# Tap matmuls of 128 contiguous weights at half-step offsets, and first loads in one ring, in a fused state-space and expert kernel

## The chip, the cores and the metric

The kernel runs on one core of one Trainium2 chip. The metric is the device time of one execution in microseconds, the median of several. A run more than 1.5% above the fastest of its kernel is called slow; with one core this label rests on the time alone. A ratio below is the mean time of one kernel's fast runs over that of the kernel before in the same rounds, so it is not quite the ratio of the medians that stand beside it. The experiments ran on several chips of one kind (the control ran on one of them); on these the kernel before had medians of 207.7 to 210.6 us, on the first chip 212.1. That spread is larger than some of the effects, so I look at the traces as well as at the times. Each trace is one execution.

Short names: PE is TensorE, ACT ScalarE, DVE VectorE, POOL the engine whose queue starts some loads, SP the engine whose queue starts most. A chunk's KT is the tap product moved out of PSUM by ACT (an **eviction**); U and K2T are the spectra of input and taps, PAB their products, which reuse the memory of AT, a table that is stored to DRAM first.

## The reference, cut to what matters

```python
xn = layernorm(u)                                         # 2048 x 512
# state-space branch: one kernel of 2048 taps per channel, used as a long convolution
P  = exp(dt * A[:, :, None] * l)                          # 512 channels x 128 states x 2048
K  = einsum("dn,dnl,dn->dl", C, P, dt * B).real
y  = irfft(rfft(xn, 4096) * rfft(K, 4096))[:2048] + xn * Dskip
# expert branch: the token with the highest router value alone goes through a small gated MLP
r  = xn @ w_r;  token = argmax(r)
xe = xn;  xe[token] += sigmoid(r[token]) * mlp(xn[token])
out = u + y * silu(xe)
```

The kernel doesn't form 2048 taps. It evaluates K at 20 centres times 32 offsets around each (GG holds the centre powers, QQ the offset powers, both complex, 128 states on the partitions) and multiplies the two with matmuls: the **tap matmuls**. The table W then carries the 640 values per channel to a spectrum.

## The kernel before

Work goes in eight **chunks** of 64 channels (two to a pair, four pairs) and four **spectra** that follow the pairs. This is one chunk:

```python
for jj in range(16):
    for ci in range(2):                                   # real, imaginary
        for gp in range(4):                               # channel groups: 4 x 32 weight columns
            mms.append((PB[32*gp:32*gp+32, 4, 20*jj:20*jj+20],
                        QQ[:, qb, ci, gp, 0:32, jj],      # 32 weights, 16 elements apart
                        GG[:, 0, ci, :, 32*gp + 16*js + jj], ci == 0, ci == 1))
...                                                       # KP product on DVE, two more matmuls
act(KT[:, js], PB[:, 4, 0:320]..., Copy, 320)             # first eviction
...                                                       # 16 + 1 "spread" matmuls with IDENT
act(KT2[...].rearrange("p t (c g) -> p g t c", g=4), PB[:, 4, 0:320]..., Copy, 320)   # second, step of 4
```

All instructions stand in a fixed order on each engine (a list, `_ORDER`), semaphores join the engines, and a list `_FILL` puts matmuls without use ("fillers") on PE to keep its clock up. X, the input, is loaded by ACT's queue; sixteen warm-up matmuls run at the start:

```python
for q in range(4):
    xl = g.dma(AC, [xsrc[q]])                             # X in four loads of 512 KB, ACT's queue
...
for k in range(4):                                        # warm-up
    g.M([(PB[:, 6 + k % 2, :], AT[:, 0, 0:128], warm, True, True) for _ in range(4)])
```

## Time and profile before

| | kernel before |
|---|---|
| median, first chip | 212.09 us (209.36 to 212.58, 4 runs) |
| profiled execution | 208.72 us, span 206.6, mean granted clock 0.878 |
| PE / DVE / ACT busy | 175.7 / 142.6 / 136.2 us |
| tap matmuls | 1024 pairs of weight load and matmul, 2.24 us per chunk |
| tap evictions per chunk | 0.44 us, then 0.88 us for the second |
| instruction blocks fetched | 25 packets, 0.41 MB |
| "issue" pauses over 1 us in the chain | 3.11 + 1.56 + 1.20 + 2.05 + 2.71 = 10.63 us |

The page gives the sums; the place of a pause is only in the chain in order of time. The lines themselves are in the prediction below.

### The profile page before, as it was taken

What the parts mean: (1) busy time and instruction counts of PE and PEld (TensorE: products, weight loads), DVE (VectorE), ACT (ScalarE), POOL (GpSimd) and SP (SyncE); (2) the same over time, 40 slices, a digit from 0 to 9 for tenths busy, and PEclk for the clock granted to TensorE, in tenths of its full rate; (3) what the DMA queues carried; (4) which work ended last, traced back from release to release, by engine and by line L of the source; (5) the groups of instructions that cost most, each with busy time, mean ns of one, the idle gap of its engine ahead of it and who ended that gap; (6) DMA issues with size and microseconds to landing.
All of it is one profiled execution on the core that took longest, in us unless ns stands there. A gap on an engine that the chain in (4) does not pass through costs nothing.

```text
span 206.6 us, 7069 instructions
## 1 busy us (share of the span) xinstructions
PE 175.7 (85%) x3170; PEld 127.9 (62%) x3181; DVE 142.6 (69%) x344; ACT 136.2 (66%) x164; POOL 13.9 (7%) x24
## 2 busy tenths in 40 slices
PE   6099998889993999967999998999999649999960
PEld 2044547555883766946898875876799327895420
DVE  1599589997970789801699999959999205542634
ACT  2059589997703978661799999986688422566431
POOL 0074000000000203000000000200002400000000
PEclk9999999995555589985999999889999757999997
DMA  6989972225595692980037297441349852366874
GB/s 176 347 272 405 415 292 84 86 83 156 138 297 185 175 293 51 408 370 8 18 87 205 75 261 198 127 112 33 75 105 306 191 123 51 94 195 178 189 167 102
DMA packets 40528, 36.85 MB, mean 178 GB/s; under 512 B 26577, under 2 KB 35922, under 8 KB 39602
## 3 DMA queue, kind: packets, MB, share of 16 engines
q1 hardware_dynamic: 37458, 20.12, 35.7%
q0 software_dynamic: 2464, 14.19, 19.5%
q10 hardware_dynamic: 576, 2.10, 3.1%
q8 instruction: 25, 0.41, 0.8%
q14 instruction: 5, 0.04, 0.1%
HBM read 25.91 MB, written 10.49 MB: 176 GB/s over the span
## 4 chain that ended last, share of the span: by engine, by line
PE 60%; ACT 12%; DVE 10%; issue 8%; DMA 7%; SPq 0%; DVEq 0%
PE PB L187 58%; DMA STG<-in_A_A_re_dram 3%; ACT U L740 3%; DMA DD<-scr_z 3%; ACT K2T L740 2%; PE PB L275 2%; DVE TT L711 2%; DVE XN L720 2%; ACT QQ L740 2%; ACT ZT L740 1%; DMA scr_z<-ZT 1%; DVE ZB L711 1%; ACT KT L740 1%; ACT XN L740 1%; DVE T L711 1%
## 5 line engine op out<-in xcount | busy, mean ns | idle before, releaser
L187 PE MATMUL PB<-KT,W 128*128 128x128 bf16 x640 | 40.1, 224 | 0.7 <-ACT KT L740 0.4
L187 PEld LDWEIGHTS PB<-KT,W 128*128 128x128 bf16 x640 | 37.3, 100 | 4.2 <-ACT KT L740 1.6
L187 PE MATMUL PB<-CA,AD 32*128 32x256 bf16 (+1 forms) x192 | 24.9, 309 | 5.7 <-DVE AD L724 5.0
L711 DVE TENSOR_TENSOR TT<-GG,ZB 128x512 bf16<-128x512 bf16 (+2 forms) x64 | 27.7, 469 | 0.4
L711 DVE TENSOR_TENSOR PAB<-U,K2T 128x1024 bf16<-128x1024 bf16 x32 | 21.3, 685 | 8.6 <-ACT K2T L740 8.6
L740 ACT ACTIVATE K2T<-PB 128x1024 bf16<-128x1024 f32 x16 | 16.5, 1034 | 14.5 <-PE PB L187 14.4
L187 PEld LDWEIGHTS PB<-CA,AD 32*128 32x128 bf16 x192 | 15.5, 114 | 15.7 <-DVE AD L724 5.9
L711 DVE TENSOR_TENSOR QQ<-QQ,EE 128x2048 bf16<-128x2048 bf16 x16 | 19.5, 1220 | 7.1 <-ACT QQ L740 7.0
L740 ACT ACTIVATE KT<-PB 128x320 bf16<-128x320 f32 x16 | 10.7, 671 | 20.2 <-PE PB L187 20.2
L187 PE MATMUL PB<-GG,QQ 128*32 128x20 bf16 x1024 | 19.8, 223 | 3.9 <-issue 3.9
L187 PEld LDWEIGHTS PB<-GG,QQ 128*32 128x32 bf16 x1024 | 18.8, 170 | 6.3 <-issue 4.3
L187 PE MATMUL PB<-PAB,FA 64*128 64x128 bf16 x512 | 17.9, 222 | 0.6 <-ACT ZT L740 0.4
L740 ACT ACTIVATE U<-PB 128x1024 bf16<-128x1024 f32 x16 | 16.3, 1037 | 2.6 <-PE PB L187 2.6
L740 ACT ACTIVATE ZT<-PB 128x1024 bf16<-128x1024 f32 x16 | 16.5, 1033 | 2.0 <-PE PB L187 2.0
L740 ACT ACTIVATE EE<-PB 128x1024 bf16<-128x1024 f32 x16 | 15.5, 1029 | 2.2 <-PE PB L187 2.2
L187 PEld LDWEIGHTS PB<-PAB,FA 64*128 64x128 bf16 x512 | 15.1, 97 | 3.0 <-ACT ZT L740 0.8
L740 ACT ACTIVATE AT<-PB 128x1024 bf16<-128x1024 f32 x16 | 16.5, 1085 | 0.7 <-PE PB L187 0.7
L711 DVE TENSOR_TENSOR TF<-PB,XN 128x512 bf16<-128x512 f32 x12 | 8.1, 686 | 11.9 <-PE PB L187 8.3
L275 PE MATMUL PB<-CA 128*128 128x512 bf16 x47 | 15.1, 439 | 1.3 <-issue 1.2
L711 DVE TENSOR_TENSOR GG<-TT 128x512 bf16<-128x512 bf16 (+2 forms) x32 | 15.0, 469 | 0.4
L187 PE MATMUL PB<-XN,CB 128*128 128x256 bf16 (+1 forms) x80 | 14.4, 314 | 0.6 <-DVE XN L720 0.5
L187 PE MATMUL PB<-BT,F2T 128*64 128x256 bf16 x128 | 11.3, 307 | 1.9 <-issue 1.6
(131 smaller groups left out, 226.7 us busy)
## 6 DMA issues: line engine op xcount, KB each, us to landing
W<-c_w POOLq DMA_DIRECT2D x4, 1280.0 KB, 9.0
scr_a<-AT SPq DMA_DIRECT2D x8, 512.0 KB, 3.6
BT<-scr_a SPq DMA_DIRECT2D x8, 512.0 KB, 5.0
scr_z<-ZT SPq DMA_DIRECT2D x16, 256.0 KB, 3.4
DD<-scr_z SPq DMA_DIRECT2D x6, 512.0 KB, 5.0
X<-in_A_u_dram ACTq DMA_DIRECT2D x4, 512.0 KB, 7.0
XR<-in_A_u_dram POOLq DMA_DIRECT2D x4, 512.0 KB, 6.3
out_dram<-XR SPq DMA_DIRECT2D x8, 256.0 KB, 3.1
```

What stands on the lines that cost most here:

```text
L187: fns.append(lambda e, o=o, l=l, r=r, st=st, sp=sp, tp=tp: e.matmul(o, lhsT=l, rhs=r, start=st, stop=sp, tile_position=tp, skip_group_chec ...
L275: n.fns = [lambda e, o=o: e.matmul(o, lhsT=lhs, rhs=rhs, start=True, stop=True, tile_position=(0, 0), skip_group_check=True)] * k
L711: g.V(lambda e: e.tensor_tensor(out=o, in0=a, in1=b, op=op), [o], [a, b], n, mode)
L720: g.V(lambda e: e.tensor_scalar(out=o, in0=a, scalar1=s1, scalar2=s2, op0=op, op1=op2), [o], ins + ([s2] if not isinstance(s2, (int, float ...
L740: nd = g.A(lambda e: e.activation(out=o, in_=i, func=func, **kw), [o], ins, n + (110 if "bias" in kw else 0), after=[ph["pre"]] if tab els ...
```

## The change

Its intent: take the offsets at half steps (0.5, 1.5, ...), so that 32 values lie evenly around a centre, and lay QQ out with channels in natural order. Then one tap matmul serves four channels with 128 contiguous weights: 32 pairs of 80 columns instead of 128 pairs of 20. Only a quarter of the 128 x 80 product is wanted; the spread matmuls pick it out. In return the first eviction is four times as large (1280 columns instead of 320, in three groups), and the second one becomes contiguous.

```diff
-            for jj in range(16):
-                for ci in range(2):
-                    for gp in range(4):
-                        mms.append((PB[32 * gp:32 * gp + 32, 4, 20 * jj:20 * jj + 20], QQ[:, qb, ci, gp, 0:32, jj], ...
+            for nj, bank in ((6, 4), (5, 5), (5, 4)):
+                mms = []
+                for k in range(nj):
+                    jj = j0 + k
+                    for ci in range(2):
+                        mms.append((PB[:, bank, 80 * k:80 * k + 80], sap(QQ, ..., [[1, 128]]),
+                                    sap(GG, ..., [[128, 20], [1, 4]]), ci == 0, ci == 1))
+                g.M(mms)
+                act(KT[:, :, j0:j0 + nj], PB[:, bank, 0:80 * nj].rearrange("p (a b) -> p b a", b=80), ACT.Copy, 80 * nj)
+                j0 += nj
...
-            act(KT2[...].rearrange("p t (c g) -> p g t c", g=4), PB[:, 4, 0:320]..., ACT.Copy, 320)
+            act(KT2[:, q, :, 64 * js:64 * js + 64], PB[:, 5, 0:320].rearrange("p (t c) -> p t c", t=5), ACT.Copy, 320)
...
-        for q in range(4):
-            xl = g.dma(AC, [xsrc[q]])
+        for q in range(5):
+            xl = g.dma(SP, [xsrc[q]])        # 256 KB first, in the same ring as A_re and the constants
...
-        g.sec = "warm"                       # the warm-up matmuls go
```

Cut away: the tables for the new offsets, the skip weight (now added by two small fp32 matmuls per half), a new `_FILL` (33 fillers instead of 57), and a whole new `_ORDER` on every engine.

## The prediction

> **What bounds the kernel now.** I read the page from the top, then the chain that ended last in order of time, then the engines' busy times by stretch, then the matmul and ScalarE (ACT) timelines around the part that changes, building the convolution kernel from its "taps".
>
> ```profile
> PE 175.7 (85%) x3170; PEld 127.9 (62%) x3181; DVE 142.6 (69%) x344; ACT 136.2 (66%) x164; POOL 13.9 (7%) x24
> ...
> q8 instruction: 25, 0.41, 0.8%
> ...
> PE 60%; ACT 12%; DVE 10%; issue 8%; DMA 7%; SPq 0%; DVEq 0%
> ...
> L740 ACT ACTIVATE KT<-PB 128x320 bf16<-128x320 f32 x16 | 10.7, 671 | 20.2 <-PE PB L187 20.2
> L187 PE MATMUL PB<-GG,QQ 128*32 128x20 bf16 x1024 | 19.8, 223 | 3.9 <-issue 3.9
> ```
>
> TensorE (PE) carries 60% of the chain. A third of all its matmuls are the 1024 tap matmuls, 20 columns each. "Issue", waiting for nothing that the profile shows, is 8% of the chain, and the tap row itself names it. In the chain by time:
>
> ```profile
> 1.20 6.41 DMA STG<-in_A_A_re_dram
> ...
> 10.07 7.85 PE PB L187 x39
> ...
> 18.25 1.91 PE PB L275 x4
> ...
> 62.08 3.11 issue
> ...
> 88.58 1.56 issue
> ...
> 93.59 1.20 issue
> ...
> 160.56 2.05 issue
> ...
> 166.20 2.71 issue
> ```
>
> The reader is to see two things. The start hangs on the load of A_re, which lands at 7.61 us. Five pauses sum to 10.63 us, each within or just after a block of 128 tap matmuls. By stretch (columns: PE, PEld, DVE, ACT, POOL busy with counts, granted clock, DMA share, GB/s):
>
> ```profile
> 47.00:62.00 15.00, 15.00 (x292) 11.35 (x292) 11.93 (x36) 7.82 (x11) 0.00 (x0) 0.50 0.66 195
> 62.00:75.00 13.00, 9.67 (x230) 6.90 (x228) 6.54 (x14) 8.26 (x11) 1.49 (x2) 0.53 0.68 201
> 110.00:133.00 23.00, 21.69 (x446) 17.41 (x444) 22.69 (x48) 22.62 (x25) 1.18 (x1) 0.98 0.61 167
> 150.00:172.00 22.00, 16.88 (x480) 13.25 (x480) 12.73 (x27) 12.84 (x17) 3.45 (x3) 0.79 0.68 170
> ```
>
> From 47 to 72 us PE is at half clock; from 110 to 133 ACT and VectorE (DVE) are both full, so there a lighter PE buys nothing.
>
> **What the Trainium skill says.** (1) "Runtime: NRT & Kernel Launch", Instruction fetch mechanics: instructions come in 16 KiB blocks of 256, the cost "mostly hidden". The trace agrees on the blocks: 0.41 MB in 25 packets is 16 KB each, and 3170 + 3181 PE instructions at 64 B are 0.41 MB. It disagrees on "hidden", as I read it: in all five pauses one q8 packet starts at most about 2 us before the pause or in its first microsecond, with the DMA busy, and PE resumes some 2 us after it. Two such blocks are 256 tap matmuls, 4.5 us of PE time. (2) "TensorE: Matmul & The Clock Gate", Weight-path perf modes: the fast weight load needs 128 weights and no fp32. The taps before load 32 strided columns, after it 128 contiguous ones. In the trace 64 pairs with 128 contiguous columns and a one-column matmul (RB,XN) take 1.89 us even at half clock, 27 ns each, so a wide load is cheap. (3) "ScalarE: Activation LUTs", What ACT_TABLE_LOAD costs: an ACTIVATE is 186 ns + 0.833 ns per element, so 453 ns for 320. The trace: the first eviction of a chunk takes 0.44 to 0.52 us, the second, which writes at a step of four elements, 0.85 to 0.89 (next fence). (4) "DMA: Bandwidth & Descriptors", Issuing engines are not separate DMA queues: all queues interleave on the same 16 engines. The trace agrees: a 128 KB load takes 6.4 us while 2 MB of X runs beside it from ACT's queue.
>
> ```profile
> 95.45 0.51 ACT L740 ACTIVATE KT<-PB 128x320 bf16<-128x320 f32 x1
> ...
> 100.18 0.88 ACT L740 ACTIVATE KT<-PB 128x320 bf16<-128x320 f32 x1
> ...
> 59.06 2.42 PE L187 MATMUL PB<-GG,QQ 128*32 128x20 bf16 x128
> 61.30 0.27 PE L187 MATMUL PB<-KP,CB 128*4 128x64 bf16 x2
> ...
> 95.67 3.55 PE L187 MATMUL PB<-KT,W 128*128 128x128 bf16 x40
> ```
>
> **The change part by part.** PE instructions fall from 3179 to 2407 matmuls, each with its load (counted in the program).
>
> *Tap matmuls.* Eight chunks. Before, 128 pairs take 61.30 - 59.06 = 2.24 us, 17.5 ns a pair, the same at both clocks. After, 32 pairs of 80 columns. The price of a pair: 40 KT,W pairs (128 columns) usually take 2.41 us at full clock, less one 0.22 us latency over 39 gaps, 56 ns; scaled by 80/128 that is 35 ns, above the 27 ns floor. 32 x 35 = 1.1 us, a gain of 1.1 per chunk at full clock; at half clock 2.2 us, no gain. Six of the eight chunks run mostly at full clock: **-6.5 us**, nearly all on the PE chain.
>
> *Spread matmuls.* Before 16 + 1 per chunk in about 0.4 us; after 20 + 1 + 2 (the two KP matmuls move here), say 0.05 us more each: **+0.4 us**.
>
> *Fetch pauses.* A chunk's tap instructions drop from 256 to 64 and their rate from one per 9 ns to one per 18. Blocks fall from 25 to 19. I expect 2 to 3 of the 10.63 us to stay: **-8 us**.
>
> *Loads.* X leaves ACT's queue; the sync ring carries 256 KB of X, the step sizes, A_re, the first constants, then the rest. 385 KB lie up to and with A_re; at the 347 GB/s of the second slice that is 1.1 us, after an issue near 1.6 us and a landing of about 2 us: A_re near 4.7 instead of 7.61. The PE order also drops the warm-up matmuls (three groups of 1.9 us between 11 and 24 us, between the exponent arguments). The new order puts fillers elsewhere. But DVE needs 16 statistics of 0.68 us = 10.9 and then the normalisations, and is full from 30 to 47. I credit 4.5 of the some 5 to 6: **-4.5 us**.
>
> *Half clock.* Fillers move to the router and the expert (57 become 33, warm-ups apart). Whether they hold the clock I can't tell: **-1.5 us**.
>
> *ACT.* A chunk's tap eviction becomes three, of 480, 400 and 400 elements: 0.58 + 0.52 + 0.52 = 1.62 us for 0.44. Its second eviction becomes contiguous: 0.44 for 0.88. The KE eviction (0.44 every second chunk) becomes one of 64 per chunk, 0.24. Net +0.76 x 8 = 6.1, and two evictions for the skip weight, 2 x 0.4: ACT goes from 136 to about 143 us. The chain runs through ACT between 117 and 142 and two chunks lie there: **+2 us**. The two skip products in fp32 (four passes of 256 columns, estimated): **+0.5 us**. DVE keeps its work but for four memsets: 0.
>
> Sum: -6.5 + 0.4 - 8 - 4.5 - 1.5 + 2 + 0.5 = -17.6. 212.5 - 17.6 = **195 us**.
>
> **The rivals.** *ACT becomes the bound.* The new tap evictions write runs of 5 or 6 bf16 values, at a step of 32 bytes. The step-4 write above costs (880 - 190)/320 = 2.2 ns per element; if short runs pay that, a chunk adds 1280 x 1.3 = 1.7 us more, 13 over eight, and ACT reaches some 156 us. For it: the 0.88 us rows, and 98% ACT in the stretch 110 to 133. Against: runs are not single elements, and ACT is idle some 40% around most chunks. About half would show: 201 us. *The pauses stay.* They may need only a busy DMA, not dense instructions: the pause at 88.58 has DMA share 1.0 all round it. Then only 2 or 3 us of the 8 come: 200 us. *DVE holds the start.* It is busy 16.93 of 17 us between 30 and 47; if its chain, not the load, sets the router's start, 2 of the 4.5 us come: 197 us. *The clock drops more often*, since with fewer tap matmuls and fillers PE idles more: each 10 us of PE work at half clock costs up to 5 us: 200 us or more. *Better than thought:* the tap chain also gets shorter, its evictions running beside the next matmul group, and the spectra start earlier: 187 us.
>
> **Range and chances.** Two rivals at once give about 206, the good one with full credit for pauses and start 186. So 195, range 186 to 206. Faster by over 2% means below 208.3, which needs most gains to fail: 0.93 faster, 0.06 same, 0.01 slower.
>
> **What would show it.** The tap row at 256 matmuls with 32 of them starting within 1.2 us at full clock (wrong: 1.8 or more); issue in the chain at or below 3% for 8; A_re landing before 5.5 us and the first argument matmul before 8; the spread evictions all at 0.44 us and the tap evictions at 0.5 to 0.6 (rival: 0.8 to 1.2); ACT busy 140 to 146 us; QQ products on DVE still at 1.22 us although their runs shrink from 256 to 16 elements. The prediction falls if ACT or DVE carries over 25% of the chain, or if the half-clock stretch grows past 25 us.

## The result, and the profile after

The changed kernel takes **200.32 us** (199.73 to 200.49, 4 runs) where the kernel before takes 212.09: ratio 0.951, 95% interval 0.942 to 0.961. Its direction and range were as predicted; by the medians it gained 11.8 us where 17.6 were expected. Two of the four runs of the kernel before count as slow; by fast runs alone the gain is 10.3 us (210.5 to 200.2). The profiled execution has a span of 198.6 us for 206.6, at a mean granted clock of 0.925 for 0.878; these two traces thus differ by 8.0 us, and only that can be followed in them.

These are the lines of the changed kernel's page that answer to those of before (busy times; fetched instructions; shares of the chain; then groups: line, engine, operation, output and inputs, count, busy us, mean ns of one, idle time before):

```profile
PE 165.8 (83%) x2411; PEld 120.2 (61%) x2411; DVE 143.5 (72%) x339; ACT 144.7 (73%) x186; POOL 13.9 (7%) x24
...
q8 instruction: 19, 0.31, 0.6%
...
PE 36%; DVE 21%; ACT 18%; DMA 17%; issue 2%; SPq 2%; DVEq 0%; ACTq 0%
...
L725 DVE TENSOR_TENSOR QQ<-QQ,EE 128x2048 bf16<-128x2048 bf16 x16 | 19.5, 1219 | 0.2
L187 PE MATMUL PB<-GG,QQ 128*128 128x80 bf16 x256 | 14.2, 213 | 1.4 <-ACT XSEL L754 0.7
```

PE lost 10 us of work and much of the chain (60% to 36%), the pauses left the chain (8% to 2%), and DMA rose from 7% to 17%. In the chain in order of time most of that DMA is one store in the expert's time:

```profile
61.33 0.37 SPq L210
61.74 1.01 SPq L210
62.79 20.52 DMA scr_a<-AT
...
83.40 0.69 DVE PAB L725
```

A store of 512 KB takes 20.5 us here, because the loads of the expert and of W run beside it (8.1 MB were moved between 57 and 80 us, from the windows' rates; in a_pool below, with one of these loads moved away, it takes 10); the products PAB are written over AT's memory, so the first of them waits for it.

More telling than any share are landmarks, the same piece of work in each trace (us; from the timelines). The control is the changed kernel once more, on a later chip; the last two columns belong to experiments below.

| landmark | before | after | control | a_all | a_best |
|---|---|---|---|---|---|
| first argument matmul | 10.1 | 6.5 | 6.9 | 6.5 | 6.5 |
| first matmul on normalised X | 30.2 | 24.9 | 24.6 | 22.2 | 24.8 |
| last of the expert's up matmuls starts | 66.7 | 56.4 | 54.5 | 56.9 | 57.1 |
| first spectrum starts on PE | 80.2 | 78.8 | 77.9 | 81.9 | 75.1 |
| second set of power products starts on DVE | 102.7 | 101.8 | 100.3 | 103.9 | 99.6 |
| first taps of the fifth chunk | 130.4 | 132.6 | 131.1 | 132.3 | 128.0 |
| third spectrum starts | 142.3 | 143.1 | 141.6 | 142.5 | 138.2 |
| fourth spectrum starts | 172.2 | 165.7 | 164.3 | 165.1 | 160.8 |
| last DD matmul group | 199.2 | 190.7 | 189.3 | 190.2 | 186.5 |
| span | 206.6 | 198.6 | 197.2 | 199.2 | 195.6 |

Read down the second and third columns. The changed kernel is 10 us ahead at 56 us, 1.4 us ahead at the first spectrum (79 us), 1 us ahead at 102, 2 us *behind* at 131, and then gains again: 7.3 us of the final 8 between the third and the fourth spectrum, where the kernel before has its last two pauses. The two stretches that decide this, by windows (columns: length; PE, PEld, DVE, ACT, POOL busy; granted clock; DMA share; GB/s), before:

```profile
102.00:124.00 22.00, 21.53 (x382) 18.53 (x383) 21.45 (x48) 21.50 (x23) 0.00 (x0) 1.00 0.56 152
124.00:131.00 7.00, 6.23 (x132) 4.31 (x128) 6.90 (x15) 7.00 (x8) 0.00 (x0) 1.00 0.73 203
160.00:172.00 12.00, 6.88 (x184) 3.85 (x179) 2.94 (x8) 4.26 (x7) 2.29 (x2) 0.62 0.61 137
```

and after:

```profile
102.00:124.00 22.00, 18.96 (x293) 14.47 (x290) 21.80 (x51) 21.45 (x24) 0.00 (x0) 1.00 0.59 172
124.00:131.00 7.00, 7.00 (x85) 4.76 (x86) 5.76 (x11) 5.40 (x6) 1.18 (x1) 0.54 0.60 169
160.00:172.00 12.00, 9.62 (x218) 8.27 (x214) 5.39 (x11) 6.76 (x12) 2.29 (x2) 1.00 0.58 133
```

From 102 to 124 DVE is full in both kernels (21.45 and 21.80 of 22 us), and ACT nearly as full (21.50 and 21.45); in the changed kernel the chain runs over DVE from 101.75 to 123.41 us. Lighter PE work buys nothing there, it only makes PE wait. After the wait PE runs at half clock from 124 to 131 (0.54), where before it ran at full clock. From 160 to 172 it is the other way round: before, the pauses left PE 6.9 of 12 us of work, and the clock fell to 0.62.

### The profile page after: what moved, and what is told of

The parts are those of the page before. It is cut to its first block, busy times and chain, and to the rows that moved or that the text cites. A ratio compares the mean times of both kernels' runs of the same rounds, so it can differ in the third digit from the quotient of the medians.

```text
span 198.6 us, 5566 instructions
## 1 busy us (share of the span) xinstructions
PE 165.8 (83%) x2411; PEld 120.2 (61%) x2411; DVE 143.5 (72%) x339; ACT 144.7 (73%) x186; POOL 13.9 (7%) x24
## 4 chain that ended last, share of the span: by engine, by line
PE 36%; DVE 21%; ACT 18%; DMA 17%; issue 2%; SPq 2%; DVEq 0%; ACTq 0%
PE PB L187 33%; DMA scr_a<-AT 10%; ACT AT L754 4%; ACT XT L957 4%; DVE TT L725 4%; DVE PAB L725 4%; ACT KT L754 4%; DMA X<-in_A_u_dram 3%; DVE ST L802 3%; DVE GG L725 2%; SPq L210 2%; DMA DD<-scr_z 2%; PE PB L280 2%; ACT K2T L754 2%; ACT QQ L754 2%
## 5 line engine op out<-in xcount | busy, mean ns | idle before, releaser
L187 PEld LDWEIGHTS PB<-KT,W 128*128 128x128 bf16 x640 | 35.9, 98 | 6.1 <-ACT K2T L754 3.4
L187 PE MATMUL PB<-CA,AD 32*128 32x256 bf16 (+1 forms) x192 | 25.9, 357 | 9.9 <-DVE AD L738 8.2
L725 DVE TENSOR_TENSOR PAB<-U,K2T 128x1024 bf16<-128x1024 bf16 x32 | 21.2, 685 | 12.8 <-ACT K2T L754 11.8
L187 PEld LDWEIGHTS PB<-CA,AD 32*128 32x128 bf16 x192 | 17.4, 129 | 16.7 <-DVE AD L738 9.1
L754 ACT ACTIVATE KT<-PB 128x400 bf16<-128x400 f32 (+2 forms) x32 | 18.4, 576 | 5.9 <-PE PB L187 5.2
L187 PE MATMUL PB<-GG,QQ 128*128 128x80 bf16 x256 | 14.2, 213 | 1.4 <-ACT XSEL L754 0.7
L187 PE MATMUL PB<-DD,CB 128*128 128x512 bf16 x32 | 10.9, 458 | 4.4 <-DVE TF L725 2.3
L187 PEld LDWEIGHTS PB<-GG,QQ 128*128 128x128 bf16 x256 | 11.9, 106 | 4.0 <-ACT XSEL L754 1.0
L187 PE MATMUL PB<-XN,CB 128*128 128x256 bf16 (+1 forms) x80 | 12.8, 297 | 1.3 <-ACT AT L754 1.3
L802 DVE BATCH_NORM_STATS2 ST<-X 128x6 f32<-128x512 bf16 x16 | 9.9, 683 | 5.1 <-DMA X<-in_A_u_dram 5.1
L280 PE MATMUL PB<-CA 128*128 128x512 bf16 x33 | 13.3, 524 | 0.1
```

The lines of the kernel that those rows point to most:

```text
L187: fns.append(lambda e, o=o, l=l, r=r, st=st, sp=sp, tp=tp: e.matmul(o, lhsT=l, rhs=r, start=st, stop=sp, tile_position=tp, skip_group_chec ...
L280: n.fns = [lambda e, o=o: e.matmul(o, lhsT=lhs, rhs=rhs, start=True, stop=True, tile_position=(0, 0), skip_group_check=True)] * k
L725: g.V(lambda e: e.tensor_tensor(out=o, in0=a, in1=b, op=op), [o], [a, b], n, mode)
L754: nd = g.A(lambda e: e.activation(out=o, in_=i, func=func, **kw), [o], ins, n + (110 if "bias" in kw else 0), after=[ph["pre"]] if tab els ...
L802: g.V(lambda e, b=b: e.bn_stats(ST[:, b, :], X0[:, b, :]), [ST[:, b, :]], [X0[:, b, :]], 512)
```

## The experiments

Twelve runs; the labels with a_ start from the changed kernel, b_ from the one before. Theory: the pauses of the instruction fetch are what the change really removes, and the rest of the gain is given back at later waits. Rivals: it is PE time that counts; the loads; ACT's larger evictions; the DMA burst.

### The loads: a_ring and b_ring

```diff
# a_ring
-            xl = g.dma(SP, [xsrc[q]])
+            xl = g.dma(AC, [xsrc[q]])
# b_ring
-            xl = g.dma(AC, [xsrc[q]])      # four pieces
+            xl = g.dma(SP, [xsrc[q]])      # five pieces, SP's order as in the changed kernel
```

> The changed kernel with one part undone: the loads of X go through the ScalarE-issued ring again instead of ahead of the others in the SyncE ring; nothing else differs. Theory A (the prediction's start term): the early start is worth what it gained at the first argument matmul, 3 to 4.5 us at the end, so about 203 to 205 us. Theory B (the lead is given back before the first spectrum, which in the changed kernel starts only 1.4 us earlier than before although the LayerNorm tail ended 10 us earlier): the first argument matmul moves from 6.5 us back towards 10 us, but the end moves by less than 1 us, 200 to 201 us.

> The kernel before with one part of the change alone: X in five pieces through the SyncE-issued ring in the changed kernel's order, warm-ups and taps as before. Theory A (prediction's start term): about 3 to 4 us faster than before, 208 to 209 us. Theory B (early lead is given back at later waits): within 1 us of before, 211 to 213 us, with the first argument matmul still some 3 us earlier than before's 10.07.

a_ring: 201.59 us, ratio 0.968 (0.960 to 0.977); the control had 0.958 (0.951 to 0.964) on the same chip. The first argument matmul moves from 6.9 to 7.9 us, but the first matmul on normalised X stays (24.7) and the last up matmul starts no later (54.6 for 54.5). It falls behind only between 55 and 80 us, in a stretch that the moved loads don't touch. So theory A's reason is not borne out by a_ring, even if a loss of up to 2 us stands in the times (more than theory B allowed). b_ring: 209.31 us against 208.73, no gain, and its first argument matmul still starts at 9.8 us. The expectation of 3 us there was a miss, and the trace says why: in the order of before a statistics instruction on X stands ahead of the last argument products on DVE and waits for X until 8.6 us. So no gain of the loads alone is shown; that DVE's new order is what they lack is my reading of that wait, and no run tests it.

### The pauses: a_narrow, a_pad, a_narrow2, a_tiny

The question is whether the gain is PE time or instruction density. a_narrow puts the density back with the real sums, a_pad puts PE time back without density:

```diff
# a_narrow
-   mms.append((PB[:, bank, 80*k:80*k+80], QQ[... 128 columns], GG[... [[128, 20], [1, 4]]]))
+   for ch in range(4):
+       mms.append((PB[32*ch: +32, 80*k + ch, step 4, 20 columns], QQ[... 32 columns], GG[... + ch, [[128, 20]]]))
# a_pad, ahead of the first group of a chunk
+   mms = [(PB[:, bank, :], IDENT, CA[:, 0:512], True, True)] * 5
```

> The changed kernel with each 128-column tap matmul split into four of a quarter of the columns: same sums, same order of everything else, but 128 pairs of matmuls per chunk as in the kernel before, so both the PE time of the taps (about 1 us more per chunk, 8 chunks) and the instruction count come back. Theory A (prediction): PE time 6.5 us and fetch pauses 8 us both return, 210 to 215 us, with one-packet instruction blocks about 25 and issue pauses of over 1 us on PE. Theory B (the pauses were off the path or hidden, only PE time counts): 204 to 207 us.

> The changed kernel with five 512-column matmuls without use put ahead of each chunk's taps: 5 x 0.216 = 1.08 us of PE more per chunk at full clock, 8.6 us in all, like the narrow taps, but with only 10 instructions more per chunk. Theory A (PE bounds the chunk loop): nearly all of it shows, 206 to 209 us, instruction blocks 19 to 21, no issue pause over 1 us; what the narrow taps lose beyond this is the fetch pauses. Theory B (the loop is bound by DVE and ACT, PE has slack): under 203 us.

a_pad: fast runs 205.94 and 205.27 us (three others were slow), ratio 0.987 (0.976 to 0.998), that is 6 us above the control's mean of 199.7 for 8.6 us of fillers. Its trace, of a slow run, has 19 blocks and no pause over 1 us on PE. PE time counts, some 70% of it; the intervals of the two ratios allow 40% to all.

a_narrow: 208.3 and 207.2 us in its fast runs, between the bands of theory B (204 to 207) and A (210 to 215), and a trap. Its DVE was busy 155.7 us instead of 143.5 and its ACT 154.0 instead of 144.7, with the same instructions. I blamed the writes to every fourth PSUM column and mended that in a_narrow2 (20 neighbouring columns, as the kernel before writes them):

> The narrow taps again, mended: the first version wrote columns 4 apart in PSUM, and DVE and ACT instructions beside its taps took up to twice their time (2.4 instead of 1.2 us). This one writes 20 neighbouring columns, as the kernel before did. Expected: DVE and ACT durations as in the changed kernel (products of 1.22 us). Then theory A (fetch pauses count): blocks 25, issue pauses over 1 us on the chain, 4 us or more above the version with five fillers per chunk, that is 9 to 12 us above the control. Theory B (only PE time counts): as the fillers, 5 to 8 us above the control, or less.

It took 212.8 and 215.8 us in its fast runs and showed the same stretching. In its timeline (start, duration):

```profile
167.24 1.02 PE L187 MATMUL PB<-GG,QQ 128*32 128x20 bf16 x45
167.34 2.06 ACT L754 ACTIVATE K2T<-PB 128x1024 bf16<-128x1024 f32 x1
167.90 1.90 DVE L725 TENSOR_TENSOR QQ<-QQ,EE 128x2048 bf16<-128x2048 bf16 x1
```

K2T normally takes 1.02 us and the product 1.22; both are stretched while the small tap matmuls run. So my reading of the first version was wrong (it wasn't the PSUM step), and neither run measures what the pauses cost. They do show something else: both fetch 25 blocks, as the kernel before, yet PE's longest pause without a wait is 0.87 us in a_narrow and under 0.35 us in a_narrow2. More blocks alone don't bring the pauses. Alone on PE, 128 narrow pairs take 2.8 us here and took 2.24 us in the kernel before; whether this lower rate is the reason is open. The kernel before has the same number of small tap matmuls and no such stretching (its products stay between 1.20 and 1.23 us); they differ in how the operands lie in memory, and which of these matters is open.

a_tiny asks again without touching QQ and GG, with 96 small matmuls on constants:

```diff
+   mms = [(PB[32*(k%4): +32, bank, 0:20], IDENT[:, 0:32], CA[:, 0:20], True, True) for k in range(96)]
```

> The changed kernel with 96 tiny matmuls (32 weight columns, 20 columns, no result that anyone uses) ahead of each chunk's taps: instruction density as in the kernel before (128 pairs per chunk), and as the narrow taps took about 20 ns a pair, some 1.9 us of PE per chunk, 15 us in all; the operands are constants, so the slowdown of DVE and ACT beside the narrow taps should be absent if it comes from reading GG and QQ in small pieces, and present if it comes from the dense stream of small matmuls itself. The version with five fillers added 8 us of PE and cost about 6 us. Theory A (fetch pauses count): blocks about 25, pauses of over 1 us on PE beyond the PE time, more than 14 us above the changed kernel (over 213 us). Theory B (only PE time counts): 9 to 12 us above (208 to 211).

It took **209.34 us**, all four runs fast: ratio 1.016, the whole gain of the change is gone. DVE and ACT keep their times (143.9 and 144.8), so the dense stream alone doesn't stretch them. The extra PE time came out smaller than I had expected, 0.85 us per chunk (134.56 to 135.41 us in the trace) and not 1.9, so 7 us in all, less than in a_pad; by a_pad's slope of 0.7 that is worth 5 us. It lost 9.8 us over the control's median and 12 us by the ratios of the fast runs (1.016 and 0.958). The rest is 5 to 7 us, and the trace has pauses of about that size. Its page, and its chain by time:

```profile
q8 instruction: 25, 0.41, 0.8%
```

```profile
57.63 0.80 issue
...
77.16 0.40 issue
...
95.76 1.39 issue
...
164.47 0.70 issue
...
167.17 1.83 issue
```

The blocks are back at 25 and the pauses with them: 0.80 + 0.40 + 1.39 + 0.70 + 1.83 = 5.1 us; PE has no such pause over 0.35 us in the control. They belong to the fetch by their time: in all ten pauses, five before and five here, one instruction packet (q8) starts 2.2 to 3.0 us before PE resumes. The numeric bands I had set fit theory B (208 to 211), but only because they assumed too much PE time; pauses present, and less PE time than a_pad at a higher total, speak for theory A. How much of the loss they are is less sure: the slope of 0.7 rests on two fast runs, and a_pad and a_tiny ran on different chips (a_store, of about the control's speed, had 199.9 us on a_tiny's). By landmarks a_tiny is 0.8 us behind the control at the first spectrum, 3.4 at the second power products, 5.1 at the third spectrum and 8.9 at the fourth. The 3.8 us between the last two hold 2.5 us of pauses and two chunks' small matmuls, 1.7 us.

### ACT's evictions: a_again (control) and a_evict

> The changed kernel itself, as the control for its variants on this chip. Nothing is changed, so about 200.3 us and 0.951 of the kernel before if the chip is like the first one; the other chip seen since ran the kernel before at 208.7 instead of 212.1, and then 197 to 199.

> The changed kernel with the taps of a chunk grouped 6, 6, 4 instead of 6, 5, 5: same matmuls, but the second eviction starts and ends on whole pairs of its target. The changed kernel's evictions took 0.57 (480 columns), 0.78 (400 columns, odd run) and 0.54 us (400 columns). Theory A (the odd run is what costs 0.78): 0.57, 0.57 and about 0.47 us, so 0.28 us less per chunk, 2.2 us of ACT in all, and 0 to 1 us off the end. Theory B (bank or order, not the odd run): the second stays near 0.78 or above, and nothing is gained.

The control: 199.59 us (198.52 to 201.21), ratio 0.958. The tap evictions of the changed kernel by form:

```profile
L754 ACT ACTIVATE KT<-PB 128x400 bf16<-128x400 f32 x16 | 10.3, 645 | 1.0 <-PE PB L187 0.5
L754 ACT ACTIVATE KT<-PB 128x480 bf16<-128x480 f32 x8 | 4.6, 570 | 2.7 <-PE PB L187 2.5
L754 ACT ACTIVATE KT<-PB 128x320 bf16<-128x320 f32 x8 | 3.6, 444 | 2.2 <-PE PB L187 2.2
```

The 400-column form takes longer than the 480-column one: half of them 0.78 us, half about 0.53. Grouped 6, 6, 4 (`for nj, bank in ((6, 4), (6, 5), (4, 4))`):

```profile
L754 ACT ACTIVATE KT<-PB 128x480 bf16<-128x480 f32 x16 | 9.3, 581 | 4.4 <-PE PB L187 4.2
L754 ACT ACTIVATE KT<-PB 128x320 bf16<-128x320 f32 x16 | 7.1, 443 | 3.0 <-PE PB L187 2.6
```

The slow form is gone, so it is the group's place and length and not the bank (the second group is still in bank 5): theory A for the duration, 2.0 us of ACT saved by these rows. (The 320 row also holds the eight spread evictions; this trace is of a slow run.) In time: 196.83 us median (193.98 to 200.27), two runs fast, ratio 0.935 (0.925 to 0.945). That is more than 2 us of ACT can give, and the next kernel that contains the same grouping, a_store, had 199.89 us and 0.960. A gain at the end is therefore not shown.

### Where the lead went: a_pool, a_store, a_all

```diff
# a_pool: POOL's order
-   ..., 19, 215, 214, 220, 235, 18, 244, ...
+   ..., 19, 18, 215, 214, 220, 235, 244, ...      # W0 ahead of WD; W0 is part of the table W
# a_store: grouping 6, 6, 4, and SP's order
-   ..., 308, 327, 323, 318, 313, ...              # the store that is ready last stands first
+   ..., 308, 327, 313, 318, 323, ...
# a_all: a_store, and the expert's last part behind the taps, in creation and on PE, ACT and DVE
-   expert(); patch(); loads of W2, W3; kpair(0)
+   expert(); kpair(0); expert_b(); patch(); loads of W2, W3
```

> The changed kernel with one load moved: W0 of the expert (issued at 58.4 us, after WD, in the changed kernel) goes out ahead of WD, as early as its memory is free, so the DMA burst of 57 to 83 us loses 1.3 MB of its 8 MB or so. Theory A (the lead of 10 us at 57 us was lost to the DMA burst: the store of AT took 18 to 20 us to land and the first PAB waited for it): the store lands earlier, the first spectrum starts 2 to 4 us earlier than 78.8 and the end comes 1 to 3 us earlier than the control. Theory B (the lead was lost to the order of work on PE, ACT and DVE in 60 to 72 us, not to DMA): the store lands earlier, but the first spectrum stays at 78 to 80 us and the end within 1 us of the control.

> The changed kernel with taps grouped 6, 6, 4 (as in the run before) and one order changed: the last three stores of AT go out in the order in which ACT finishes them; in the changed kernel the last one to be ready, at 61.3 us, stands first and holds the two others, which then land only at 83.35 us in the DMA burst, and the first PAB products, in AT's memory, wait for that. Theory A (that wait held the first spectrum): no such wait on the chain, first PAB matmul 1 us or more earlier than 83.9 to 84.3, end 1 to 2 us below the 6, 6, 4 version (which was at 0.935 of the kernel before). Theory B (K2T, from the taps by way of PE and ACT, comes at the same time anyway): first PAB matmul within 0.7 us, end within 1 us.

> As the run before it (6, 6, 4 and stores in order of readiness), and the expert's last part and the patch go behind the taps of the first two chunks in the order of every engine, two fillers dropped. Theory A (the 10 us lead at 57 us was lost because the patch, which waits for WD until 65 us, stands ahead of the taps): the spread of the second chunk ends some 8 us earlier, the first spectrum starts at 69 to 73 us instead of 77.6 to 78.8, and the end comes 3 to 6 us earlier: 191 to 194 us where the changed kernel has 199.6. Theory B (the DMA burst of 57 to 83 us or DVE's chains hold the spectra anyway): the first spectrum starts earlier, but the first product of the fourth chunk pair's taps and the end move by less than 1.5 us.

a_pool (W0 is not an expert's load, as its expectation calls it): 200.50 us beside the control's 199.59. The last three stores land in 8 to 10 us where the control's take 17 to 20, and yet nothing starts earlier: first spectrum at 79.4 us, first PAB matmul at 85.8 (control: 77.9 and 84.3). a_store: 199.89 us, ratio 0.960; the store is off the chain, yet the first PAB matmul starts at 84.8 us, no earlier than in the control. Both say theory B: the 20 us wait for the store that the chain showed was real in that execution, but K2T and the order of work bring PAB to the same time without it. The control's chain has no such wait either and its landmarks are the same.

a_all was meant to gain 3 to 6 us and took 200.89 us, ratio 0.973, its first spectrum at 81.9 us instead of 69 to 73. I had put argument matmuls ahead of the second chunk's spread, and they waited for ACT:

```profile
71.50 1.88 PE L187 MATMUL PB<-CA,AD 32*128 32x256 bf16 x8 [3.67 <-ACT QQ L760]
```

PE idled 3.67 us and ran at half clock after it; the expert's last matmuls took 4.9 us for 2.3 (75.01 on). The mistake still taught something. a_all starts the second power products 3.6 us later than the control, yet reaches the fifth chunk's taps 28.4 us after (132.3 - 103.9) instead of 30.8, at full clock throughout. So the half-clock stretch at 124 to 131 us costs the changed kernel about 2.4 us. Other traces mostly fit: in nine of them PE waits 1.76 to 2.31 us for DVE at 119 to 126 us, and in eight of these 6.8 to 10.2 us at half clock follow. The ninth, a_narrow (1.94 us), keeps its clock, and so does a_all with waits of 1.23 and 1.32 us, but a_pool loses 3.4 us of clock after one of 0.84. The length of the wait alone doesn't decide it.

### The version that these point to: a_best

The grouping and store order as above, the expert's last part behind the taps without the mistake, and a `_FILL` entry of seven matmuls where PE waits at 120 us:

```diff
-   (129, 4, 2), (216, 2, 6)]
+   (129, 4, 2), (134, 4, 7), (216, 2, 6)]
```

> The version that the runs so far point to: taps grouped 6, 6, 4; stores of AT in order of readiness; the expert's last part behind the taps of the first two chunks, this time without the mistake of the first attempt (there the spread of the second chunk stood behind argument matmuls that waited for ACT, PE idled 4 us in 67 to 74 us and fell to half clock, and the second set of power products began on DVE at 103.9 us instead of 100 to 101); and seven fillers in the 1.8 us that PE waits at 120 us, after which it ran at half clock from 123 to 130 us in the changed kernel. Two separate readings of the trace. Front: theory A says the second set of power products on DVE starts at 95 to 98 us, theory B (DMA or DVE hold the first spectrum anyway) at 99.5 to 101. Clock: theory A says full clock from 120 to 131 us and 28 to 29.5 us from the start of those products to the first taps of the fifth chunk (31 to 32.6 in the changed kernel), theory B (DVE bounds this stretch, PE's clock does not matter) still 31 or more. End: both A, 191 to 194 us; one of them, 194.5 to 197.5; both B, 198 to 200.

It takes **197.73 us** (195.51 to 200.01, 6 runs), ratio 0.954 (0.941 to 0.966); its five fast runs average 197.2, those of the control 199.7 on another chip. It beats the kernel before clearly and the changed kernel by about 1%, which the intervals of the ratios don't separate. The two readings:

```profile
102.00:124.00 22.00, 20.45 (x298) 14.81 (x291) 21.79 (x50) 21.44 (x24) 0.00 (x0) 1.00 0.58 177
124.00:131.00 7.00, 6.48 (x103) 4.23 (x102) 6.97 (x12) 6.97 (x10) 1.18 (x1) 1.00 0.55 143
```

*Clock*: theory A. The granted clock is 1.00 in both windows and the fifth chunk's taps come 28.4 us (128.0 - 99.6) after the power products, as in a_all. The filler closes the gap; but a_all, of nearly the same order, kept the clock and the 28.4 us without it, so that the filler is needed, or does it alone, is not shown. *Front*: theory B. The first spectrum starts 2.8 us before the control's, the power products only 0.7 us. What holds the stretch from 80 to 100 us was not settled: DVE is nearly full from 85 to 95 us in both kernels, but only 1.4 (changed kernel) and 2.0 us (a_best) busy of the 5 after that.

## Why the prediction was right or wrong

**Tap matmuls, -6.5 us.** Mechanism right: at full clock 12 and 20 pairs take 0.54 and 0.83 us to the start of what follows (from 132.59 and 133.69 us), so 1.37 us for 32, between the 1.2 hoped for and the 1.8 that would have refuted it: 43 ns a pair and not 35. Six chunks then gain 6 x (2.24 - 1.37) = 5.2 us, and by a_pad some 70% of PE time reaches the end, not "nearly all": an estimate of 3.7.

**Fetch pauses, -8 us.** Right in kind, and the best supported step: blocks 25 to 19, issue 8% to 2%, and a_tiny brings blocks and pauses back. One reading was loose: the pause at 88.58 us comes 3 us after its chunk's taps ended (85.60), behind 40 spectrum matmuls. The size was off because I credited pauses by their length and not by their place. The three of 62 to 94 us, 5.87 us together, lie ahead of 102 us, where 1 us of all lead is left. The two at 160 and 166 us, 4.76 us, lie between the third and fourth spectrum, where the changed kernel gains 7.3 us and the clock gained too (0.62 to 1.00). a_tiny agrees for the late pauses only: its delays ahead of 102 us did not vanish (3.4 us of some 6, pauses and small matmuls together).

**Loads, -4.5 us.** A_re is used at 4.6 us and the first argument matmul starts at 6.5, both as predicted; 5.3 us of lead are there at the first matmul on normalised X, 10 at 56 us. This step failed in its last clause, "I credit 4.5 of the some 5 to 6": 1 us is left at 102 us, although three pauses and four chunks of taps lie ahead of it too. My rival "DVE holds the start" did not come either: the lead still grew after DVE's full stretch (30 to 47 us) and was lost between 56 and 79 us.

**Half clock, -1.5 us.** The mean clock rose by 0.047, but a new half-clock stretch of 7 us appeared behind a wait of 2.3 us on PE, and cost about 2.4 us. The prediction had this as a rival ("the clock drops more often") and gave it no place.

**ACT, +2 us.** 144.7 us busy, inside 140 to 146. The rival of expensive short runs fell, except for one of three evictions (0.78 us); a chunk's tap evictions take 0.57 + 0.645 x 2 = 1.86 us for the 1.62 of the sum. The second eviction is at 0.44 as said, KE 0.20 for 0.24. **fp32 skip products, +0.5:** four, of 0.38 to 0.59 us each; the two at full clock start 0.21 us apart. **DVE 0:** the KP product went from 0.22 to 0.37 us, perhaps because its operand is now strided (not tested); the QQ products stayed at 1.22.

So 17.6 became 11.8 (10.3 by fast runs) because terms were added at full length that did not reach the end. Two losses are seen. The lead of 10 us at 56 us is down to 1.4 at the first spectrum; this comes before the stretch that DVE fills, and what absorbs it is open: an earlier store (a_pool, a_store) did not bring it back, a_best's order brought 2.8 us at the first spectrum and 0.7 at the power products. And from there to the fifth chunk's taps the changed kernel needs 30.8 us for the 27.7 before, 2.4 of it half clock. That the time fell inside the range doesn't confirm the sum: 186 to 206 allowed gains of some 6 to 26 us.

## What to carry to other kernels

Follow landmarks, not shares: list when the same ten pieces of work start in both traces, and a gain that is given back shows itself at once. Credit a removed wait by what lies between it and the end: here 10 us of lead at 56 us were 1 us at 102. Less PE work in a stretch in which another engine is full buys nothing (27.7 us before from the second power products to the fifth chunk's taps, 28.4 at best after): PE waits, and in eight of nine traces here a wait of about two microseconds was followed by seven to ten at half clock. Fillers in that gap are worth a try; that they alone help is not shown.

## What the Trainium skill lacked or had wrong

- "Runtime: NRT & Kernel Launch", Instruction fetch mechanics, calls the cost of a block "mostly hidden". With 256 PE instructions per chunk in small matmuls the pauses were 1.2 to 3.1 us each in the kernel before, 10.63 us in all, and 0.4 to 1.8 us in a_tiny; with 64 per chunk, none over 0.35 us. With 256 per chunk and as many blocks, but slower taps, a_narrow's longest was 0.87 us and a_narrow2 had none over 0.35.
- "SBUF — State Buffer", Who interferes with whom, says that only DVE and GpSimd contend, and that "PE and ACT never wait on anyone". Beside the small tap matmuls of a_narrow2 an ACT eviction took 2.06 us for 1.02 and a DVE product up to 2.39 for 1.22; DVE was busy 155.5 us for 143.5. The cause is open, and so is whether it lies in SBUF (the eviction reads PSUM).
- "TensorE: Matmul & The Clock Gate", HAM oscillation, gives the rule "no PE-idle gaps >~3.4µs". Here gaps of 2.31 us (changed kernel) and 1.76 us (a_evict) were followed by about 7 us at half clock; two of 1.2 and 1.3 us in a_all were not, nor one of 1.94 us in a_narrow.
- "ScalarE: Activation LUTs", What ACT_TABLE_LOAD costs, has 186 ns + 0.833 ns per element for an ACTIVATE with immediate scale and bias and no term for the output pattern, so 519 ns for 400 (an estimate by it). The step-4 write took 0.88 us for 320 elements and the five-element runs of the second group 0.78 us for 400, those of the third 0.53.
